# k and v from batch 3 on with four tokens to a partition: 40 k-v matmuls of mostly 128 rows in place of 72 of 64 rows

## The chip, the cores and the metric

The kernel runs on one core of one Trainium2 chip. The metric is the device time of one execution in microseconds (us); smaller is better. Executions that agree are called fast runs; one execution of the kernel before took 524 us and is left out of every comparison.

## The reference, cut to what matters

```python
# q, k, v: (8 batches, 8 heads, 576 tokens, 64)
q_s = softmax(q, over the 64 features)
k_s = softmax(k, over the 576 tokens)
kv  = einsum('bhsd,bhse->bhde', k_s, v)       # the k-v products
out = einsum('bhsd,bhde->bhse', q_s, kv)
# then out, as 4608 x 512, goes through silu(x @ w_in) @ w_out, w_in 512 x 2048
```

The k-v products are small: 64 by 64 per head. Most of the work is in the two large products behind them.

## The kernel before

The large products run by a scheme of seven products for eight, for which VectorE forms sums and differences of operand blocks (the tiles S, T, XS, WS, and GT in place). One batch of attention is worked into each stage of 26 us of large products: ScalarE takes exponentials of q and k, GpSimd casts v to bf16 (into `vaug`, which has a column for the softmax sum) and normalises q, a DMA transposes q (tile qT), TensorE makes the k-v products (`kv`) and later multiplies q with them (`xt`).

A load brings four heads as two pairs. Head r of a pair lies on partitions 64 r to 64 r + 63, nine tokens to a partition. So a k-v product contracts 64 partitions and runs on a quarter (64 rows by 64 columns) of TensorE's array:

```python
P, J = 64, S // 64                      # 64 partitions per head, 9 tokens each
x = src[b].rearrange("(g r) (p j) d -> g (r p) (j d)", r=2, j=J)
eng.dma_start(out=t, in_=x.rearrange("g x y -> x g y")[:, 2 * cc:2 * cc + 2, :])
...
def kv(b, cc):                          # cc: which half of the heads
    for j in range(J):
        for r in range(2):              # row half of the array
            for s in range(2):          # column half of the array
                nc.tensor.matmul(
                    out=PS[s * 64:(s + 1) * 64, 6 + r, cc * 128:cc * 128 + E1],
                    lhsT=ek[r * 64:(r + 1) * 64, j, (2 * cc + s) * D:(2 * cc + s + 1) * D],
                    rhs=vaug[r * 64:(r + 1) * 64, j, 2 * cc + s, :],
                    start=(j == 0), stop=(j == J - 1))
```

That is 9 x 2 x 2 = 36 matmuls for each half of the heads, 72 a batch.

The softmax here doesn't subtract the row's maximum and nothing guards it: scores larger than these inputs give would overflow.

Of the kernel before, what the change touches and what calls it, by code (L numbers as in the profile page):

```python
# [11 lines left out]
ACT = mybir.ActivationFunctionType  # L12
# [5 lines left out]
def kernel(  # L18
# [9 lines left out]
    nc = tc.nc  # L28
    B, H, S, D = q.shape
    DM, DFF = w_in.shape  # L30
    NT = B * S
    P = 64
    J = S // P
# [8 lines left out]
    E1 = D + 1  # L42
# [24 lines left out]
    vaug = glob.tile([128, J, NG, E1], BF16, name="vaug")  # L67
    ek = glob.tile([128, J, NG * D], BF16, name="ek")
# [5 lines left out]
    PS = ps.tile([128, 8, 512], FP32, name="PS")  # L74
# [10 lines left out]
    st = [dict() for _ in range(B)]  # L85

    def copy(eng, o, i):
        if eng is nc.scalar:
            eng.copy(out=o, in_=i)  # L89
        else:  # L90
            eng.tensor_copy(o, i)  # L91

    def load(b, name, src, cc, eng):
        t = ld.tile([128, 2, J * D], FP32, name=name)
        st[b][name, cc] = t
        x = src[b].rearrange("(g r) (p j) d -> g (r p) (j d)", r=2, j=J)
        eng.dma_start(out=t, in_=x.rearrange("g x y -> x g y")[:, 2 * cc:2 * cc + 2, :])

    def jgd(b, name, cc):
        return st[b][name, cc].rearrange("p g (j d) -> p j g d", d=D)  # L100

    def half(t, cc):
        return t[:, :, cc * 128:(cc + 1) * 128].rearrange("p j (g d) -> p j g d", d=D)
# [6 lines left out]
        )  # L110

    def exp_k(b, cc):
        nc.scalar.activation(out=half(ek, cc), in_=jgd(b, "kt", cc), func=ACT.Exp)  # L113

    def vcast(b, cc, eng, g0=0, g1=2):
        o = vaug[:, :, 2 * cc + g0:2 * cc + g1, 0:D]
        i = jgd(b, "vt", cc)[:, :, g0:g1, :]
        copy(eng, o, i)
# [66 lines left out]
    def kv(b, cc):  # L185
        for j in range(J):
            for r in range(2):
                for s in range(2):
# [4 lines that stand above are left out]
                        start=(j == 0),  # L193
                        stop=(j == J - 1),
                    )

    def kvcopy(b, c0=0, c1=2):
        kp = PS[:, 6:8, 0:256].rearrange("p r (c x) -> p r c x", x=128)[:, :, c0:c1, 0:E1]
        rz = ap.tile([128, 2, 2], FP32, name="rz", bufs=2)[:, :, 0:c1 - c0]
        nc.vector.reciprocal(out=rz, in_=kp[:, :, :, D])  # L200
        for c in range(c0, c1):
            nc.vector.tensor_tensor(
                out=kvn[b % 3][:, c],
                in0=kp[:, :, c - c0, 0:D],
                in1=rz[:, :, c - c0, None].to_broadcast([128, 2, D]),
                op=ALU.mult,
            )

    def kv_both(b):
        kv(b, 0)  # L210
        kv(b, 1)
        kvcopy(b)

    def pieces(t):
# [315 lines left out]
    for name, src in (("qt", q), ("kt", k)):  # L530
        load(0, name, src, 0, nc.sync)
        if name == "qt":
            load(0, name, src, 1, nc.sync)
    load(0, "vt", v, 0, nc.sync)
    load(0, "kt", k, 1, nc.sync)
    load(0, "vt", v, 1, nc.sync)
# [38 lines left out]
    qnorm(0, 0, nc.vector)  # L575
    qsum(0, 1)
    exp_k(0, 0)
    tr(0, 0, 0, 5, 0)
    tr(0, 0, 5, J, 1)
    heat(7)  # L580
    qnorm(0, 1, nc.vector)
    vcast(0, 0, nc.scalar)
    trcopy(0, 0, 0, 5, 0, nc.scalar)
    trcopy(0, 0, 5, J, 1)
    kv(0, 0)
    kvcopy(0, 0, 1)
    tr(0, 1, 0, 5, 2)
    tr(0, 1, 5, J, 3)
    exp_k(0, 1)
    xt_mm(0, 0, 0, 320, 4, 0)  # L590
    xt_mm(0, 0, 320, 256, 0, 0)
    heat(3, 6)
    vcast(0, 1, nc.scalar, 0, 1)
    vcast(0, 1, nc.vector, 1, 2)
    trcopy(0, 1, 0, 5, 2, nc.scalar)
    trcopy(0, 1, 5, J, 3)
    kv(0, 1)
    kvcopy(0, 1, 2)
    heat(2, 3)
    xt_evac(0, 0, 4, 0, 320, 0, nc.scalar)  # L600
# [47 lines left out]
    def full(t):  # L648
# [17 lines left out]
        for i in range(2):  # L666
            plan(u + (3, 10)[i], lambda i=i: exp_q(b, i))
            plan(u + (7, 11)[i], lambda i=i: qsum(b, i))
            plan(u + (16, 17)[i], lambda i=i: qnorm(b, i, nc.gpsimd))
            plan(u + (2, 11)[i], lambda i=i: vcast(b, i, nc.gpsimd))  # L670
            plan(u + (6, 4)[i], lambda i=i: exp_k(b, i))
            if more:
                plan(u + (5, 12)[i], lambda i=i: load(b + 1, "qt", q, i, nc.sync))
                plan(u + (8, 6)[i], lambda i=i: load(b + 1, "kt", k, i, nc.sync))
                plan(u + (22, 23)[i], lambda i=i: load(b + 1, "vt", v, i, nc.sync))
        plan(u + 17, lambda: q_transpose(b))
        plan(u + 15, lambda: kv_both(b))
        plan(u + 22, lambda: xt(t + 1, 0, nc.vector))
        plan(u + 27, lambda: xt(t + 1, 1))
# [98 lines left out]
    plan(b1 + 5, lambda: (vcast(1, 1, nc.scalar, 0, 1), vcast(1, 1, nc.vector, 1, 2)))  # L778
    plan(b1 + 6, lambda: (trcopy(1, 1, 0, 5, 0, nc.scalar), trcopy(1, 1, 5, J, 1)))
    plan(b1 + 7, lambda: kv_both(1))  # L780
    plan(b1 + 8, lambda: xt(1, 0))
    plan(b1 + 9, lambda: xt(1, 1))
# [20 lines left out]
    plan(b1 + 13, lambda: ws_op(1, 0))  # L803
    plan(b1 + 24, lambda: ws_op(2, 0))
    plan(b1 + 25, lambda: kv_both(2))
    plan(b1 + 24, lambda: t_op(2, nc.vector))
    plan(b1 + 27, lambda: xt(2, 0, nc.vector))
# [42 lines left out]
```

## Time and profile before

| what | before |
|---|---|
| median of its four runs, the 524 us run among them | 263.19 us |
| span of the profiled run | 260.8 us |
| TensorE busy | 252.4 us, 97% |
| VectorE busy | 207.3 us, 79% |
| one stage of large products, batches 4 to 7 | 26.2 us |
| the 72 k-v matmuls inside it | 0.83 us |

How to read it: TensorE is the bound, and work added to it in a stage without gaps moves the end by as much. The lines that show this stand in the prediction. Two more views of before are needed later. First the timeline in the stretch where batch 3 arrives (start us, length us, engine, line, operation, out<-in; the bracket is the idle time before and what ended it):

```profile
64.18 2.12 POOL L91 CAST vaug<-vt 128x1152 bf16<-128x1152 f32 x1 [9.03 <-DMA vt<-in_v_dram]
66.62 1.17 POOL L91 CAST vaug<-vt 128x1152 bf16<-128x1152 f32 x1 [0.32 <-DMA vt<-in_v_dram]
...
64.06 1.22 DVE L452 TENSOR_TENSOR W<-W 128x2048 f16<-128x2048 f16 x1
...
68.89 1.23 DVE L442 TENSOR_TENSOR S<-S,GT 128x2048 f16<-128x2048 f16 x1
```

GpSimd's casts of v follow their loads at once. VectorE's operations with two SBUF inputs take 1.22 us.

Second, the windows view of the loads' stretch (window, length, busy times of PE, PEld (weight loads), DVE (VectorE), ACT (ScalarE), POOL (GpSimd), clock, DMA share, GB/s):

```profile
59.00:67.00 8.00, 7.88 (x67) 5.64 (x66) 7.90 (x12) 7.39 (x10) 2.50 (x2) 1.00 1.04 388
```

The transfers run at 388 GB/s with every DMA engine taken.

### The profile page before, as it was taken

To read this page: it belongs to the slowest core of one execution; us is meant where nothing else is said; L and a number is where in the kernel's file an instruction comes from. 1 tells how busy PE (TensorE), PEld (TensorE's weight loads), DVE (VectorE), ACT (ScalarE), POOL (GpSimd) and SP (SyncE) were. 2 spreads that over 40 slices of the span, in tenths; PEclk is the share of its full clock that TensorE was granted. 3 is DMA by queue.
4 is the path that set the end of the run, shared out by engine and by line. 5 is a ranking of instruction groups with operands and counts; after the bars stand their busy time and mean duration, and the time that the engine had idled before them with its cause. 6 is when DMAs were issued, how large, how long until landed. Compare 5 with 4: busy or idle time off the path is not lost.

```text
span 260.8 us, 6412 instructions
## 1 busy us (share of the span) xinstructions
PE 252.4 (97%) x2732; PEld 203.0 (78%) x2732; DVE 207.3 (79%) x268; ACT 187.6 (72%) x212; POOL 66.9 (26%) x62
## 2 busy tenths in 40 slices
PE   8799999999999999999999999999999999999993
PEld 3457756656887888888888888888888888888882
DVE  2967786879997999799979997999798548855832
ACT  5767877998994799579956996699664757584710
POOL 1753691741360306030603060306000000000004
PEclk9999999999999999999999999999999999999999
DMA  7999999689979477957784879640424002500534
GB/s 248 334 198 298 298 323 333 253 186 384 309 284 222 123 209 247 197 146 201 258 220 118 214 249 152 182 104 3 90 61 102 3 0 46 117 3 1 120 84 121
DMA packets 35452, 45.89 MB, mean 176 GB/s; under 512 B 16208, under 2 KB 19984, under 8 KB 35424
## 3 DMA queue, kind: packets, MB, share of 16 engines
q1 hardware_dynamic: 29488, 33.63, 47.2%
q0 software_dynamic: 5616, 11.60, 16.9%
q8 instruction: 21, 0.34, 0.5%
q10 hardware_dynamic: 320, 0.26, 0.4%
q14 instruction: 7, 0.06, 0.1%
HBM read 36.70 MB, written 9.44 MB: 177 GB/s over the span
## 4 chain that ended last, share of the span: by engine, by line
PE 80%; DVE 12%; ACT 2%; POOL 2%; DMA 1%; issue 1%; POOLq 0%; DVEq 0%; ACTq 0%
PE PS L468 34%; PE PS L368 32%; PE PS L405 5%; PE PS L258 3%; PE PS L228 2%; DVE zq L148 2%; PE PS L189 2%; DVE h L346 2%; DMA qt<-in_q_dram 1%; PE PS L276 1%; DVE eq L157 1%; DVE GT L442 1%; DVE S L442 1%; ACT eq L108 1%; POOL out_dram L730 1%
## 5 line engine op out<-in xcount | busy, mean ns | idle before, releaser
L346 DVE TENSOR_TENSOR h<-PS,h 128x1024 f32<-128x1024 f32 (+1 forms) x45 | 53.9, 1199 | 12.0 <-PE PS L368 6.0
L468 PEld LDWEIGHTS <-GT 128*128 128x128 f16 x512 | 49.5, 98 | 6.9 <-issue 1.2
L368 PEld LDWEIGHTS <-WS 128*128 128x128 f16 x480 | 46.8, 98 | 7.5 <-issue 1.4
L468 PE MATMUL PS<-W,GT 128*128 128x256 f16 x384 | 49.1, 273 | 0.0
L368 PE MATMUL PS<-XS,WS 128*128 128x256 f16 (+1 forms) x360 | 46.3, 272 | 0.6 <-DVE h L346 0.5
L352 ACT ACTIVATE GT<-h 128x1024 f16<-128x1024 f32 (+1 forms) x45 | 46.1, 1047 | 0.3 <-DVE h L346 0.3
L89 ACT COPY h<-PS 128x1024 f32<-128x1024 f32 (+1 forms) x35 | 35.1, 1003 | 13.9 <-PE PS L368 13.4
L157 POOL TENSOR_TENSOR eq<-eq,rzq 128x1152 bf16<-128x1152 bf16 x13 | 27.7, 2134 | 57.6 <-DVE rzq L152 56.1
L468 PEld LDWEIGHTS <-S 128*128 128x128 f16 x384 | 37.1, 98 | 5.5 <-issue 1.0
L368 PEld LDWEIGHTS <-W 128*128 128x128 f16 x360 | 34.7, 98 | 4.8 <-issue 0.5
L468 PE MATMUL PS<-T,S 128*128 128x256 f16 x256 | 32.7, 273 | 0.1
L368 PE MATMUL PS<-XT,W 128*128 128x256 f16 (+1 forms) x240 | 29.5, 272 | 0.1
L352 ACT ACTIVATE GT<-PS 128x1024 f16<-128x1024 f32 (+1 forms) x15 | 15.2, 1016 | 18.9 <-PE PS L368 18.9
L91 POOL CAST vaug<-vt 128x1152 bf16<-128x1152 f32 x12 | 15.8, 1322 | 43.3 <-DMA vt<-in_v_dram 41.1
L730 POOL DMA_DIRECT2D out_dram<-ow x5 | 2.7, 546 | 72.1 <-DVE ow L715 72.1
L108 ACT ACTIVATE eq<-qt 128x1152 bf16<-128x1152 f32 (+1 forms) x18 | 19.0, 1057 | 2.5 <-DMA qt<-in_q_dram 2.4
L113 ACT ACTIVATE ek<-kt 128x1152 bf16<-128x1152 f32 x16 | 18.4, 1153 | 1.2 <-DMA kt<-in_k_dram 1.2
L148 DVE TENSOR_REDUCE zq<-eq 128x18 f32<-128x1152 bf16 x12 | 16.1, 1344 | 3.8 <-ACT eq L108 3.8
L258 PE MATMUL PS<-XT,W 128*128 128x288 f16 x128 | 16.3, 286 | 0.5 <-DVE XT L91 0.2
L468 PE MATMUL PS<-W,S 128*128 128x256 f16 x128 | 16.5, 273 | 0.0
L488 DVE SCALAR_TENSOR_TENSOR ow<-PS,sc 128x512 f32<-128x512 f32 x7 | 4.8, 691 | 14.4 <-ACT sc L484 14.4
L258 PEld LDWEIGHTS <-W 128*128 128x128 f16 x128 | 12.4, 98 | 4.3 <-issue 1.3
(78 smaller groups left out, 346.0 us busy)
## 6 DMA issues: line engine op xcount, KB each, us to landing
out_dram<-ow SPq DMA_DIRECT2D x64, 128.0 KB, 2.4
qt<-in_q_dram SPq DMA_DIRECT2D x12, 576.0 KB, 4.4
kt<-in_k_dram SPq DMA_DIRECT2D x12, 576.0 KB, 5.5
vt<-in_v_dram SPq DMA_DIRECT2D x12, 576.0 KB, 5.4
qt<-in_q_dram POOLq DMA_DIRECT2D x4, 576.0 KB, 10.3
kt<-in_k_dram POOLq DMA_DIRECT2D x4, 576.0 KB, 13.9
vt<-in_v_dram POOLq DMA_DIRECT2D x4, 576.0 KB, 13.2
W<-in_moe_w_out_dram POOLq DMA_DIRECT2D x4, 512.0 KB, 15.0
```

The costliest lines, as they stand in the source:

```text
L89: eng.copy(out=o, in_=i)
L91: eng.tensor_copy(o, i)
L108: nc.scalar.activation(out=half(st[b]["eq"], cc)[:, :, g0:g1], in_=jgd(b, "qt", cc)[:, :, g0:g1], func=ACT.Exp)
L113: nc.scalar.activation(out=half(ek, cc), in_=jgd(b, "kt", cc), func=ACT.Exp)
L148: nc.vector.reduce_sum(out=z, in_=e, axis=AX.X)
L157: eng.tensor_tensor(out=e, in0=e, in1=r[:, :, :, None].to_broadcast([128, J, 2, D]), op=ALU.mult)
L258: nc.tensor.matmul(out=PS[:, 2 * (fb % 3) + n, 0:S // 2], lhsT=W1[:, c, fb * 128:(fb + 1) * 128], rhs=XTS[0][:, c, n * (S // 2):(n + 1) * ...
L346: nc.vector.tensor_tensor(out=four(t, i), in0=group_bank(t, True), in1=four(t, i), op=ALU.add)
L352: nc.scalar.activation(out=group_out(t, f, n), in_=x, func=ACT.Silu, scale=1.0 / XS)
L368: nc.tensor.matmul(out=PS[:, bank + p // 2, (p % 2) * HT:(p % 2) * HT + width(t)], lhsT=a[:, c, p * 128:(p + 1) * 128], rhs=bb[:, c, 0:wid ...
L405: nc.tensor.matmul(out=PS[:, 2 + tb, :], lhsT=GTS[t % 2][:, fc, tb * 128:(tb + 1) * 128], rhs=W2[:, fc, :], start=(fc == 0), stop=(fc == N ...
L468: nc.tensor.matmul(out=PS[:, bank, m * HN:(m + 1) * HN], lhsT=a[:, fc, m * 128:(m + 1) * 128], rhs=bb[:, fc, :], start=(first and fc == 0) ...
```

## The change

The intent is fewer TensorE instructions: with a head's tokens over all 128 partitions, four to a partition, a product contracts 128 rows. 576 is 4 x 128 + 64, so the last 64 tokens of each head stay on 64 partitions: per half of the heads 4 x 4 wide matmuls and 4 narrow ones. Only batches 3 to 7 change.

```diff
+    JT = S // 128
+    def tall(b):
+        return b >= 3
     def load(b, name, src, cc, eng):
...
+        if tall(b) and name != "qt":
+            f = flat(t)
+            x = src[b][4 * cc:4 * cc + 4]
+            eng.dma_start(
+                out=f[:, 0:4 * JT * D].rearrange("p (h x) -> p h x", h=4),
+                in_=x[:, 0:JT * 128, :].rearrange("h (p j) d -> p h (j d)", j=JT),
+            )
+            x = x[:, JT * 128:S, :].rearrange("(g r) p d -> r p g d", r=2)
+            for r in range(2):
+                eng.dma_start(
+                    out=f[r * P:(r + 1) * P, 4 * JT * D:].rearrange("p (g d) -> p g d", g=2),
+                    in_=x[r],
+                )
+            return
...
+    def kv_tall(cc):
+        for j in range(JT + 1):
+            for r in range(2):
+                for s in range(2):
+                    rows = slice(0, 128) if j < JT else slice(r * P, (r + 1) * P)
+                    i = cc * 2 * J + ((2 * s + r) * JT + j if j < JT else 4 * JT + s)
+                    nc.tensor.matmul(
+                        out=PS[s * 64:(s + 1) * 64, 6 + r, cc * 128:cc * 128 + E1],
+                        lhsT=flat(ek)[rows, i * D:(i + 1) * D],
+                        rhs=vslot(i)[rows],
+                        start=(j == 0),
+                        stop=(j == JT),
+                    )
```

The exponentials of k and the casts of v run in flat order over the same 1,152 elements (cut here).

More of the change, by code (lines that the diff above doesn't have):

```diff
@@ L91, in copy, with flat @@
             eng.tensor_copy(o, i)
+    JT = S // 128
+    def tall(b):
+        return b >= 3
+    def flat(t):
+        return t.rearrange("p a b -> p (a b)")
     def load(b, name, src, cc, eng):
@@ L112, in exp_k, with vslot @@
     def exp_k(b, cc):
+        if tall(b):
+            nc.scalar.activation(
+                out=flat(ek)[:, cc * J * 128:(cc + 1) * J * 128],
+                in_=flat(st[b]["kt", cc]),
+                func=ACT.Exp,
+            )
+            return
         nc.scalar.activation(out=half(ek, cc), in_=jgd(b, "kt", cc), func=ACT.Exp)
+    def vslot(i):
+        return vaug.rearrange("p j g e -> p (j g) e")[:, i, :]
     def vcast(b, cc, eng, g0=0, g1=2):
+        if tall(b):
+            o = vaug.rearrange("p j g e -> p (j g) e")[:, cc * 2 * J:(cc + 1) * 2 * J, 0:D]
+            copy(eng, o, flat(st[b]["vt", cc]).rearrange("p (i d) -> p i d", d=D))
+            return
         o = vaug[:, :, 2 * cc + g0:2 * cc + g1, 0:D]
@@ L195, in kv @@
                     )
+    def kv_tall(cc):
[10 more added lines that the diff above has]
+                        stop=(j == JT),
+                    )
     def kvcopy(b, c0=0, c1=2):
@@ L209, in kv_both @@
     def kv_both(b):
-        kv(b, 0)
-        kv(b, 1)
+        for cc in range(2):
+            if tall(b):
+                kv_tall(cc)
+            else:
+                kv(b, cc)
         kvcopy(b)
```

## The prediction

> **What bounds the kernel now.** I read the page first (busy shares, chain of waits), then the windows view by stage, then the timeline around one batch's k-v products, then the waits.
>
> ```profile
> PE 252.4 (97%) x2732; PEld 203.0 (78%) x2732; DVE 207.3 (79%) x268; ACT 187.6 (72%) x212; POOL 66.9 (26%) x62
> ...
> PE 80%; DVE 12%; ACT 2%; POOL 2%; DMA 1%; issue 1%; POOLq 0%; DVEq 0%; ACTq 0%
> PE PS L468 34%; PE PS L368 32%; PE PS L405 5%; PE PS L258 3%; PE PS L228 2%; DVE zq L148 2%; PE PS L189 2%; DVE h L346 2%; DMA qt<-in_q_dram 1%; PE PS L276 1%; DVE eq L157 1%; DVE GT L442 1%; DVE S L442 1%; ACT eq L108 1%; POOL out_dram L730 1%
> ```
>
> TensorE is busy 97% of the span and is 80% of the chain that ended last. L189, the line that the change touches, has 2% of that chain, for eight batches. Five of them (3 to 7) change. So even taking their products away altogether is worth under 2%.
>
> The windows view, with the columns PE, PEld, DVE, ACT, POOL, then clock, DMA share and GB/s, shows where a TensorE saving or loss counts:
>
> ```profile
> 76.00:81.00 5.00, 4.51 (x82) 3.89 (x70) 4.97 (x7) 3.67 (x4) 1.61 (x1) 1.00 0.60 137
> 81.00:102.40 21.40, 21.40 (x205) 18.33 (x203) 19.11 (x23) 17.27 (x18) 5.28 (x4) 1.00 0.77 218
> 102.40:128.60 26.20, 26.20 (x313) 22.65 (x312) 23.76 (x29) 21.19 (x22) 6.56 (x5) 1.00 0.75 199
> 128.60:154.80 26.20, 26.20 (x313) 22.65 (x312) 23.76 (x30) 21.19 (x22) 6.56 (x5) 1.00 0.72 201
> ```
>
> From 81 us on, TensorE has no gap in a stage of 26.20 us: what is added to it there comes out at the end. In 76 to 81 us VectorE is the full engine. The chain in order of time says the same of batch 3's stage:
>
> ```profile
> 76.06 2.63 DVE GT L442
> 79.22 1.22 DVE h L346
> 80.48 1.03 PE PS L368 x8
> ```
>
> Batch 3's products run at 75.59 us, inside this VectorE stretch; the matmul at 80.48 had waited 0.49 us for VectorE (timeline). That batch can lose some 0.5 us on TensorE free of charge. The products of batches 4 to 7 lie at about 102, 129, 155 and 181 us, where TensorE is the bound.
>
> Now the stage itself, in the timeline (start, length, engine, what; the bracket is idle time before):
>
> ```profile
> 99.72 1.04 PE L368 MATMUL PS<-XT,WS 128*128 128x256 f16 x8
> ...
> 100.59 1.04 PE L468 MATMUL PS<-T,S 128*128 128x256 f16 x8
> ...
> 101.47 1.04 PE L368 MATMUL PS<-XT,W 128*128 128x256 f16 x8
> ...
> 102.43 0.69 PEld L189 LDWEIGHTS <-ek 64*64 64x64 bf16 x72 [0.21 <-issue]
> 102.43 0.81 PE L189 MATMUL PS<-vaug,ek 64*64 64x65 bf16 x72
> ```
>
> ```profile
> 103.17 1.05 PE L368 MATMUL PS<-XT,W 128*128 128x256 f16 x8
> 104.68 0.17 DVE L200 RECIPROCAL rz<-PS 128x4 f32<-128x4 f32 x1
> ```
>
> ```profile
> L189 PE MATMUL PS<-vaug,ek x576: 188/193/216, 10.9 to 181.6; 64*64 64x65 bf16 x192
> ```
>
> Groups of eight full matmuls start 0.875 us apart (99.72, 100.59, 101.47), which is 109 ns a matmul of 256 columns, or 0.43 ns a column. Without the products the next group would start at 102.34; it starts at 103.17. **So a batch's 72 products cost 0.83 us**, not 72 times their 193 ns. It splits in three. Entry: 102.34 to 102.43, 0.09 us. Stream: busy 0.81 less the last matmul's own 0.216 (the longest in the tile view) is 0.594 us from first start to last start, so 8.4 ns a matmul, or 33 ns for a round of four. Exit: the last starts at 103.03, streams 65 columns (65 x 0.43 = 28 ns) and the next group starts at 103.17, so 0.11 to 0.12 us. The 72 already run four abreast: 28 ns of streaming in a 33 ns round.
>
> **What the Trainium skill says.** "TensorEngine Tiling (Array Packing)", Key Properties: changing the tiling mode, "not just tile", drains the engine, and tiles work independently. The trace agrees with both: the 0.09 and 0.11 us at the ends, and four products in 33 ns. Its Available Configurations list 128x64 (two tiles) and 64x64 (four tiles) as separate modes; I take a step between them to be a mode change too, which nothing before the change shows. "TensorE: Matmul & The Clock Gate", Part 3, What overlaps and what doesn't: a weight load overlaps a matmul in flight only where the row group differs. The trace does not agree for the full-array matmuls: they use all rows, their loads have a median near 98 ns, yet they start every 109 ns, which is the stream alone. The new matmuls use all 128 rows as well, so I take their loads as hidden, with a doubt that I price below. "DMA: Bandwidth & Descriptors", Specifications, gives 512 B as the least transfer for line rate; no load before the change is in such small pieces, so no trace here shows what they cost.
>
> **The change, part by part.**
> (a) Matmuls. The order of instructions on each engine shows that TensorE loses 160 weight loads and 160 matmuls (32 in each of five batches) and that nothing else there moves. The 72 were 18 rounds of four 64x64 tiles. The new form has, for each half of the heads, 16 matmuls of 128 rows by 64 columns of the array, of which only two can be abreast: 8 rounds; then four of 64x64: 1 round. Two halves: 18 rounds. The array work is the same as before; the count falls only because each matmul takes twice the array. At 28 ns (stream alone) to 33 ns (round as now) the 16 wide rounds take 0.45 to 0.53 us, the two narrow ones 0.07: 0.52 to 0.60 us against 0.594. Saving per batch 0 to 0.07 us.
> (b) Mode steps. Before: into 64x64 and out of it. After: into 128x64, to 64x64, back to 128x64 for the second half, to 64x64, out. Three more, each some 0.10 us (the mean of 0.09 and 0.115): +0.30 us.
> (c) Sum per batch: +0.23 to +0.30, say +0.27 us. Batches 4 to 7 pay in full: 4 x 0.27 = 1.1 us. Batch 3 pays nothing, within its 0.49 us.
> (d) ScalarE's exponentials and GpSimd's casts have the same 1,152 elements a partition and the same count, only in flat order. Nothing. The products' result is read at 104.68, 1.4 us after they end: a late end does not show on VectorE.
> (e) Loads. Each of 20 k and v loads goes from one issue (256 pieces of 2,304 B) to three (512 pieces of 1,024 B, 256 of 256 B).
>
> ```profile
> 103.70 3.29 SPq L167 DMA_TRANSPOSE qT<-eq  x1
> 107.04 1.09 SPq L97 DMA_DIRECT2D vt<-in_v_dram  x2
> 114.09 6.09 SPq L401 DMA_DIRECT2D out_dram<-ow  x8
> ```
>
> An issue takes SyncE about 0.5 us (1.09 for two), so eight more in a stage are some 4 us on a queue that is busy about 15 of 26 us. Two v loads become six issues, 107.0 to 110.2, before the stores' 114.1. Landing now comes at 111.2 and 112.6, the casts follow at 111.3 and 112.8, and their reader is the next batch's products at 128.6: 14 us of slack. k loads are issued at 121 to 123 and read at 146. Both hidden. The tight place is batch 3's first loads: they are issued from 55 to 58 us in a stretch where the transfers are the limit, and the last of them, the second q half, lands at 67.9 and is read by ScalarE at 70.2. I estimate 0.3 us more for each of the four k and v loads before it, so 69.1: still in time, and perhaps 0.3 us if the semaphores that the issues share make SyncE wait. I put 0.2 us on it.
>
> Sum: 262.9 + 1.1 + 0.2 = **264.2 us**.
>
> **The rivals.**
> 1. *Fewer matmuls, less time* (the change's intent). If the 8.4 ns were a cost of issuing each matmul and not of the array, 40 would take 0.34 us and with no further mode cost each batch would save 0.25 us: 4 x 0.25, so 261.9 us. For it: 33 ns is more than the 28 ns of streaming, so issuing does bind a little. Against it: two wide matmuls abreast cannot stream 65 columns in less than 28 ns.
> 2. *Column halves don't overlap or weight loads show.* If the wide matmuls run one by one, 32 x 28 to 33 ns is 1.0 us in place of 0.53, so +0.5 on top of +0.3: 0.8 us in each of four or five batches, 266.3 us. If each weight load (64 columns, estimated at 28 ns like a stream) shows as well, 32 x 60 ns, +1.7 us a batch: 270 us. For it: the skill's sentence on row groups, and no 128x64 matmul in this trace. Against it: the full-array loads are hidden, and 64x64 tiles side by side on the same rows do overlap.
> 3. *The transfers become the bound* in 55 to 76 us, where the DMA share is 1.00 at the end. If small pieces take twice as long, the second q half is 2 to 3 us late, ScalarE waits, then VectorE: 265 to 267 us. For it: the small pieces. Against it: only a ninth of the bytes is in them, and later stages have a DMA share of 0.75 and over 10 us of slack.
>
> **Range and chances.** Rival 1 gives the low end, 261.9; half a miss of rival 2 or 3 gives the high end, 267. A gain over 2% (5.3 us) is impossible by the stage's whole cost of 5 x 0.83 = 4.2 us. A loss over 2% needs 1.3 us in each of four batches, which only unhidden loads or a bad stall reach: 6%.
>
> **What would show it.** The stage at batch 4: next full group 1.05 to 1.15 us later than it would start without the products, against 0.83 now, with breaks of about 0.1 us inside it between wide and narrow matmuls; wide ones 14 to 17 ns apart. A stage of about 26.5 us, not 26.2. Casts and exponentials of batches 4 to 7 still without a wait that TensorE feels. It is wrong if the inner breaks are absent (then the time falls), if the wide matmuls lie 30 ns or more apart (rival 2), or if ScalarE or VectorE waits on q, k or v near 66 to 76 us (rival 3).

## The result, and the profile after

The changed kernel took 264.97 us in the median of four runs (264.77 to 265.15). Ratios here are the mean time of one kernel's fast runs over that of the other's of the same rounds, so not quite the ratio of the medians quoted. The ratio is 1.0074, interval 1.0051 to 1.0098. Repeated in five rounds (e12 below), it was 264.88 against 263.23 us, ratio 1.0062, interval 1.0046 to 1.0078. So the change costs 1.6 to 2.0 us. It is slower, clear of noise, but by less than 1%.

The page of the changed kernel, busy line and chain by engine:

```profile
PE 254.7 (97%) x2572; PEld 204.2 (78%) x2572; DVE 207.9 (79%) x268; ACT 187.6 (71%) x212; POOL 66.3 (25%) x62
...
PE 84%; DVE 9%; ACT 2%; POOL 2%; DMA 1%; issue 1%; POOLq 0%; DVEq 0%; ACTq 0%
```

TensorE has 160 matmuls fewer and is busy 2.3 us more. Now the stage of batch 4 in the timeline, beside the lines of before in the prediction:

```profile
102.08 1.04 PE L423 MATMUL PS<-XT,W 128*128 128x256 f16 x8
103.05 1.13 PE L241 MATMUL PS<-vaug,ek 128*64 128x65 bf16 x40
104.11 1.05 PE L423 MATMUL PS<-XT,W 128*128 128x256 f16 x8
```

By the prediction's rule the next full group would have started at 102.08 + 0.875 = 102.95; it starts at 104.11. The products cost 1.16 us in place of 0.83. The single records of the stage give the starts of the 40 matmuls (ns from the first; computed from the trace):

```
16 wide, first half     0 .. 248     pairs: first to second 53 apart, then 29 to 36
4 narrow                373 .. 383   373 - 248 = 125 after the last wide one
16 wide, second half    528 .. 779   528 - 383 = 145 after the last narrow one
4 narrow                903 .. 913   903 - 779 = 124
before: 72 narrow       0 .. 593     rounds: first to second 53 apart, then 29 to 40; no break
```

So the matmuls themselves are no faster: a pair of wide ones takes what a round of four narrow ones took, 32 ns in the mean after the first step. And there are three breaks of 0.12 to 0.15 us, start to start, where an ordinary step is 0.03; before had none. First to last start, 0.913 us against 0.593: +0.32 us in a batch.

Following the products' start from batch to batch shows where the rest comes from (single records, us):

| batch | before | after | difference |
|---|---|---|---|
| 3 | 75.59 | 76.54 | +0.95 |
| 4 | 102.43 | 103.05 | +0.62 |
| 5 | 128.62 | 129.57 | +0.94 |
| 6 | 154.82 | 156.08 | +1.26 |
| 7 | 181.01 | 182.60 | +1.59 |
| a group of W,S matmuls near the end | 243.17 | 245.11 | +1.94 |

From batch 4 on, each stage adds 0.32 us, four times 1.3 us. The other 0.62 us is there before batch 4. At batch 3 it was 0.95, some of which the stage behind it took back. This 0.62 us rests on one trace of each kernel, and traces that load batch 3 in the old way differ among themselves: batch 4's products start at 102.30 us in e10, 102.43 in before, 102.83 in e1 and 103.08 in e5. The ratios of e2 and e6 below are the better evidence that batch 3 costs about half a microsecond. The timeline of the changed kernel shows what happened ahead of batch 3:

```profile
66.76 1.15 POOL L91 CAST vaug<-vt 128x1152 bf16<-128x1152 f32 x1 [11.60 <-DMA vt<-in_v_dram]
68.58 1.42 POOL L91 CAST vaug<-vt 128x1152 bf16<-128x1152 f32 x1 [0.66 <-DMA vt<-in_v_dram]
...
69.02 2.05 DVE L497 TENSOR_TENSOR S<-S,GT 128x2048 f16<-128x2048 f16 x1
...
71.12 1.05 PE L523 MATMUL PS<-T,S 128*128 128x256 f16 x8 [1.02 <-DVE S L497]
```

The casts come 2.6 and 2.0 us later than before, because v landed later. The second now runs beside VectorE's S operation, which takes 2.05 us in place of 1.23, and TensorE waits 1.02 us for it; its group starts at 71.12 us, where in before it started at 70.17. The loads' stretch in the windows view:

```profile
59.00:67.00 8.00, 7.88 (x68) 5.64 (x66) 7.90 (x12) 7.41 (x10) 0.24 (x1) 1.00 1.12 290
```

290 GB/s in place of 388, with the DMA engines as busy. The loads were also issued later. An issue is the instruction by which SyncE starts a transfer. Here are those of the two v loads in before, and below them in the changed kernel:

```profile
56.57 1.22 SPq L97 DMA_DIRECT2D vt<-in_v_dram  x2
...
59.48 0.52 SPq L109 DMA_DIRECT2D vt<-in_v_dram  x1
60.05 1.65 SPq L115 DMA_DIRECT2D vt<-in_v_dram  x2
61.86 0.48 SPq L109 DMA_DIRECT2D vt<-in_v_dram  x1
62.38 1.97 SPq L115 DMA_DIRECT2D vt<-in_v_dram  x2
```

Single records put the last v issue at 63.15 us, 5.9 us later than in before (57.27), and its landing at 68.43 us, 2.0 us later (66.47). A 32 KB issue of v took 4.4 us to land in this run's median. So, as an estimate, this one would have landed at about 67.5 us at the usual pace: SyncE's issuing may make half of the delay, the lower rate the rest. No run separates the two.

**How GpSimd can stop VectorE.** The Trainium skill, "SBUF — State Buffer", section "SBUF: two separate sides", says that VectorE and GpSimd share one pair of SBUF ports under an exclusive lock: a VectorE operation with two SBUF inputs and a GpSimd operation that reads SBUF exclude each other for the whole instruction, and the one that starts first gets it. The traces agree, in both directions. Alone, VectorE's 128x2048 operations of this kind take 1.22 us. Where GpSimd was already at work they ended 1.07 to 1.08 us after GpSimd's end, however long that took: 2.05 us (the S operation above), 2.35 and 2.71 us (the in-place GT operation of batch 3's stage, changed kernel and before). The lines of before for the last:

```profile
75.49 2.12 POOL L157 TENSOR_TENSOR eq<-eq,rzq 128x1152 bf16<-128x1152 bf16 x1 [1.49 <-ACT GT L352]
75.97 2.71 DVE L442 TENSOR_TENSOR GT<-GT 128x2048 f16<-128x2048 f16 x1
```

GpSimd ends at 77.61 us, VectorE at 78.68. And before's first cast, 0.12 us behind VectorE's W operation, took 2.12 us where others take 1.15.

### The profile page after: what moved, and what is told of

Read it like the earlier page. It is cut to its first block, busy times and chain, and to the rows that moved or that the text cites. A ratio compares the mean times of both kernels' runs of the same rounds, so it can differ in the third digit from the quotient of the medians.

```text
span 263.2 us, 6154 instructions
## 1 busy us (share of the span) xinstructions
PE 254.7 (97%) x2572; PEld 204.2 (78%) x2572; DVE 207.9 (79%) x268; ACT 187.6 (71%) x212; POOL 66.3 (25%) x62
## 4 chain that ended last, share of the span: by engine, by line
PE 84%; DVE 9%; ACT 2%; POOL 2%; DMA 1%; issue 1%; POOLq 0%; DVEq 0%; ACTq 0%
PE PS L523 35%; PE PS L423 33%; PE PS L460 5%; PE PS L313 3%; PE PS L283 2%; PE PS L241 2%; DMA qt<-in_q_dram 1%; DVE S L497 1%; PE PS L331 1%; DVE eq L195 1%; DVE zq L186 1%; ACT eq L132 1%; PE PS L227 1%; POOL out_dram L785 1%; DVE XT L91 1%
## 5 line engine op out<-in xcount | busy, mean ns | idle before, releaser
L91 POOL CAST vaug<-vt 128x1152 bf16<-128x1152 f32 x12 | 15.0, 1255 | 52.1 <-DMA vt<-in_v_dram 46.2
L460 PE MATMUL PS<-W,GT 128*128 128x512 f16 x64 | 15.6, 379 | 0.0
```

What stands on the lines that cost most here:

```text
L91: eng.tensor_copy(o, i)
L460: nc.tensor.matmul(out=PS[:, 2 + tb, :], lhsT=GTS[t % 2][:, fc, tb * 128:(tb + 1) * 128], rhs=W2[:, fc, :], start=(fc == 0), stop=(fc == N ...
```

## The experiments

**Theory A**: mode steps inside the products cost 0.32 us in each of batches 4 to 7, and late v loads cost batch 3 some 0.6 us through the port. Rivals: all from the loads (B), all from the matmuls (C), the new matmuls slow in themselves (D), the long S operation not caused by the cast (E). A mode step is a change from one tile shape of the array to another. "The S operation" is the second of the two that VectorE makes near 69 us. A gain or loss in us is the ratio less one, times the median of before; landing times and starts with three places are single records of the trace. Kernels e1 to e4 ran on one chip, e5 to e8 on a second, e9 to e12 on a third, each beside runs of before.

### e1: new matmuls on old loads

```diff
-        if tall(b) and name != "qt":
+        if False and name != "qt":
```

> The changed kernel's 40 matmuls on tiles that the old loads fill (wrong values on purpose: tokens of two heads are mixed; the work on every engine but the load queue is that of the changed kernel). Theory A (mode steps on TensorE cost the batches 4 to 7 some 0.32 us each, the smaller load pieces cost the rest through batch 3): batch 3's products start at 75.6 us again, no wait for VectorE at 70 us, each stage of batches 4 to 7 is 26.5 us, the sum +1.3 us over the kernel before, so about 264.2 us. Rival B (the loads make the whole loss, the matmuls none): equal to the kernel before, 262.9 us. Rival C (the matmuls make the whole loss): +1.8 us, 264.9 us.

Measured: ratio 1.0054 (1.0034 to 1.0075), 264.51 against 263.12 us, so +1.4 us. First to last start was 0.913 us again and the stages of batches 4 to 7 took 26.515 us each. The S operation took 1.23 us; batch 3's products started at 75.99 us and batch 4's at 102.83, 26.83 us later, as long as before (26.85), so batch 3's own 0.32 us was swallowed by VectorE's stretch, as predicted. B falls: the matmuls alone cost most of the loss. C's +1.8 us lies inside the interval (0.9 to 2.0 us), near its upper end; this run alone does not exclude it, e2 and e6 speak against it.

### e2: new loads under the old matmuls

```diff
         for cc in range(2):
-            if tall(b):
-                kv_tall(cc)
-            else:
-                kv(b, cc)
+            kv(b, cc)
```

> The changed kernel's loads, exponentials and casts with the old 72 matmuls of 64x64 (wrong values on purpose: the tokens lie elsewhere than these matmuls take them from; the time is unaffected by values). Theory A: the products' stage is 0.59 us from first to last start and a full stage 26.2 us, but VectorE's S operation near 69 us is held up by GpSimd's cast again and batch 3's products start near 76.5 us; +0.5 to +0.6 us over the kernel before, 263.4 us. Rival B: +1.8 us. Rival C: no loss.

Measured: ratio 1.0021 (1.0004 to 1.0038), +0.55 us. The products' first to last start was 0.585 us, the later stages 26.17 us, and the S operation took 2.05 us, all as A says. The profiled run was its slowest, 265.88 us (the others 263.4 to 264.1): in it, TensorE also waited 2.1 us for batch 3's transposed q. So the loads can hurt at a second place. The recorded ratio is about that of the six other runs; with the profiled run in, the plain mean is 0.9 us over before's. By the ratios e1 and e2 together make 1.95 us, the loss of the whole change, but with these intervals the agreement is a loose one.

### e3: the wide matmuls of both halves first, then the narrow ones

```diff
-    def kv_tall(cc):
-        for j in range(JT + 1):
+    def kv_tall(cc, js):
+        for j in js:
...
-                        start=(j == 0),
+                        start=(cc == 0 and j == 0),
...
+            for js in (range(JT), (JT,)):
+                for cc in range(2):
+                    kv_tall(cc, js)
```

(Only the first group in a bank may carry the start flag here, for both halves accumulate in the same banks at once.)

> The changed kernel with the order of its 40 matmuls altered: the 32 wide ones of both halves first, then the eight narrow ones, so one mode step inside in place of three; right values. Theory A (each inner step costs some 0.11 us): first to last start 0.68 us in place of 0.91, stages of 26.28 us in place of 26.52, about -1.1 us against the changed kernel, 263.9 us. Rival D (wide matmuls or narrow ones are slow in themselves, whatever their order): first to last start stays at 0.91 us and the time at 265.0 us.

Measured: right result, first to last start 0.691 us, stages of 26.274 us. The timeline of batch 4:

```profile
101.88 1.04 PE L426 MATMUL PS<-XT,W 128*128 128x256 f16 x8
102.85 0.89 PE L241 MATMUL PS<-vaug,ek 128*64 128x65 bf16 x40
103.67 1.05 PE L426 MATMUL PS<-XT,W 128*128 128x256 f16 x8
```

The same 40 matmuls in another order cost 103.67 - 102.76 = 0.91 us in place of 1.16. D falls: two breaks fewer make 0.22 to 0.25 us. The time, 264.48 us and ratio 1.0044 (1.0026 to 1.0063), is +1.2 us over before, where 263.9 us was expected. The profiled run, 263.61 us, was the fastest of six (the others 264.1 to 265.1). What the others lost is not in a trace.

### e4: no narrow matmuls

```diff
-                    rows = slice(0, 128) if j < JT else slice(r * P, (r + 1) * P)
+                    rows = slice(0, 128)
```

> The changed kernel with the eight narrow matmuls made wide too (wrong values on purpose: the last 64 tokens of two heads are mixed), so that there is no mode step inside at all. Theory A: 20 pairs at 31 ns, first to last start 0.62 to 0.65 us, stages of 26.25 us, 263.7 us. It also gives the price of a pair alone: were wide matmuls faster than the old 64x64 rounds, this would be below the old 0.59 us. Rival D (wide matmuls slow in themselves): 0.9 us or more.

Measured: first to last start 0.630 us, that is 20 pairs, 53 ns for the first step and 32 for the later ones in the mean; ratio 1.0024 (1.0008 to 1.0041), +0.6 us. No break is left inside, so the breaks come with the change of shape. It is not below the 0.593 us of before, but the comparison in the expectation is not a fair one: eight narrow matmuls made wide are four pairs in place of two rounds, so e4 streams 20 rounds where before and the change stream 18. Round for round the two are equal, 32 ns each. This is the answer to the change's intent: a pair of double size is no faster than four matmuls that run abreast.

### e5: only batches 4 to 7 changed; e6: only batch 3 changed

```diff
-        return b >= 3
+        return b >= 4        # e5;  b == 3 in e6
```

> The changed kernel with batch 3 left in the old layout and only batches 4 to 7 tall; right values. Theory A (the inner mode steps cost 0.32 us in each of batches 4 to 7, and batch 3's crowded loads cost about 0.5 us apart from them): batch 3's products start at 75.6 to 76.0 us, no wait for VectorE's S operation near 70 us, +1.3 us over the kernel before, 264.3 us. Rival C (TensorE alone makes the loss, and the late start of batch 3 is a matter of the single run): as the changed kernel, +1.8 us.

> Only batch 3 tall; right values. Theory A: batch 3's v lands 1.5 to 2 us later, GpSimd's cast meets VectorE's S operation, its products start near 76.5 us, its own 0.32 us are partly absorbed, and all later stages are 26.2 us: +0.5 to +0.6 us over the kernel before, 263.6 us. Rival C: +0.3 us at most.

Measured, e6: ratio 1.0017 (1.0001 to 1.0033), +0.45 us; the S operation 2.05 us; later stages 26.19 us. As A says. Its timeline also has the wait:

```profile
68.39 1.18 POOL L91 CAST vaug<-vt 128x1152 bf16<-128x1152 f32 x1 [1.18 <-DMA vt<-in_v_dram]
68.59 2.05 DVE L497 TENSOR_TENSOR S<-S,GT 128x2048 f16<-128x2048 f16 x1
...
70.70 1.05 PE L523 MATMUL PS<-T,S 128*128 128x256 f16 x8 [0.69 <-DVE S L497]
```

Measured, e5: ratio 1.0073 (1.0057 to 1.0089), +1.9 us, where 1.3 was expected: a miss. The S operations were short, the stages 26.515 us as expected, but batch 3's products started at 76.24 us. The timeline shows why:

```profile
63.82 1.22 POOL L91 CAST vaug<-vt 128x1152 bf16<-128x1152 f32 x1 [8.79 <-DMA vt<-in_v_dram]
...
63.94 2.17 DVE L507 TENSOR_TENSOR W<-W 128x2048 f16<-128x2048 f16 x1
...
67.30 1.03 PE L423 MATMUL PS<-XS,WS 128*128 128x256 f16 x8 [1.07 <-DVE h L401]
```

Here the first cast started 0.12 us *before* VectorE's W operation and so took the port; in the trace of before it was 0.12 us *behind* and lost it. This loss comes from nothing in the edit: batch 3's loads are the old ones. Whether the unprofiled runs of e5 lost the port too is not shown.

### e7: v ahead of the second k half in batch 3's loads

```diff
-        ("qt", q, 0), ("kt", k, 1), ("kt", k, 0), ("vt", v, 0), ("vt", v, 1), ("qt", q, 1)
+        ("qt", q, 0), ("kt", k, 1), ("vt", v, 0), ("vt", v, 1), ("kt", k, 0), ("qt", q, 1)
```

> The changed kernel with the first block of loads (batch 3) in another order: q, k half, v, v, k half, q, so that v lands 2 to 3 us earlier. Right values. Theory A: GpSimd's casts end before 67.5 us, VectorE's two S operations take 1.2 us each (1.5 and 2.05 in the changed kernel), the wait of 1.0 us on TensorE at 70 us is gone, batch 3's products start near 75.6 us, about -0.5 us against the changed kernel, 264.4 us. Rival E (the S operation is long for another reason than the cast beside it, such as the transfers' writes): it stays at 2 us and the time at 265.0 us.

Measured: the cast was out of the way, both S operations took 1.21 and 1.23 us, and batch 3's products started at 75.45 us, earlier than in before. The lines of e7:

```profile
64.45 3.03 POOL L91 CAST vaug<-vt 128x1152 bf16<-128x1152 f32 x2 [9.23 <-DMA vt<-in_v_dram]
67.51 1.21 DVE L497 TENSOR_TENSOR S<-GT 128x2048 f16<-128x2048 f16 x1
68.75 1.23 DVE L497 TENSOR_TENSOR S<-S,GT 128x2048 f16<-128x2048 f16 x1
```

E falls. But the time did not get better, where a gain of 0.5 us was expected: 265.18 against 262.65 us, ratio 1.0090 (1.0074 to 1.0106), a miss. What was won at 70 us was given back at 83 us:

```profile
82.73 0.28 PE L283 MATMUL PS<-qT,kvn 64*64 64x192 bf16 x4
83.73 0.33 PE L283 MATMUL PS<-qT,kvn 64*64 64x320 bf16 x4 [0.73 <-DMA qT<-eq]
```

Batch 3's transposed q landed at 83.7 us (82.3 in before). It shares the transfers with batch 4's k and q, whose last load landed at 81.7 us in place of 77.4 in before. So the slow loads set two limits for batch 3 that lie within a microsecond of each other, and removing the first uncovers the second.

### e8 and e11: before, with VectorE's GT operation moved out of GpSimd's way

```diff
-        for i, x in ((1, 4), (2, 5), (3, 15), (4, 19)):
+        for i, x in ((1, 4), (2, 5), (3, 18 if t == 2 else 15), (4, 19)):   # e8
```

> The kernel before, with one VectorE operation (the third S operation of the stage in which batch 3 is worked on) three units of work later, after GpSimd's second normalisation instead of beside it. Right values. If VectorE really stands still while GpSimd works on such an operation, it takes 1.22 us in place of 2.71 us, TensorE's wait of 0.49 us for VectorE near 80 us goes, and the kernel ends 0.3 to 0.5 us earlier than the kernel before: 262.5 us. If it doesn't, nothing changes, or TensorE waits for the late operation and it is slower.

Measured: the GT operation (the third S operation of the expectation) took 1.22 us in place of 2.71, but it now ran too late: TensorE waited 0.77 us for it in place of 0.49 for the h addition. Ratio 1.0025 (1.0005 to 1.0045): +0.65 us, a miss; the expectation had named this way to fail. e11 puts the same operation between the scaling of the products and the h addition:

> The kernel before, with batch 3's third S operation put behind the scaling of its k-v products in VectorE's queue instead of ahead of it, and ahead of the next h addition. Right values. VectorE then does the 0.7 us of scaling while GpSimd normalises, and waits less: the S operation takes about 1.5 us in place of 2.7, TensorE's wait of 0.49 us near 80 us shrinks to under 0.2, and the kernel is 0.3 to 0.4 us faster than before, 262.3 us, if the transpose of batch 3 is not the next limit; if it is, no change.

Measured: 262.94 against 263.23 us, ratio 0.9981 (0.9962 to 1.0): perhaps 0.5 us faster, not settled. Runs lie from 262.03 to 264.42 us. The profiled run was the slowest one; there the GT operation took 1.61 us as expected, but the whole run was 1.6 us late by 44 us, and the cast again got the port 0.08 us ahead of the W operation, which took 2.17 us.

### e9: old layout, loads cut into three issues

```diff
+        if b >= 3 and name != "qt":
+            eng.dma_start(out=t[:, 0], in_=y[:, 0])
+            for r in range(2):
+                eng.dma_start(out=t[r * P:(r + 1) * P, 1], in_=y[r * P:(r + 1) * P, 1])
+            return
```

> The kernel before, with each k and v load from batch 3 on cut into three issues as in the changed kernel (one of 128 partitions, two of 64), but still in pieces of 2,304 B. Right values. Theory F (the small pieces slow the transfers): batch 3's last v half lands near 66.5 us as before, the rate in 59 to 67 us stays near 390 GB/s, the time is that of the kernel before, 262.7 us. Rival G (the 20 times two more issues delay the loads): v lands near 68 us, VectorE's S operation is held up by the cast, and batch 4's second q half and the transpose come late as in the changed kernel: +0.5 us.

Measured: 267.43 against 263.23 us, ratio 1.0150 (1.0126 to 1.0174), +3.9 us, twice the loss of the change itself. But the four unprofiled runs had a granted clock of 0.991 to 0.992, before's 0.996 to 1.0; the profiled run, at 0.997, took 265.94 us, 2.7 us over before's median. So over a microsecond of the 3.9 may be of clock. The windows view and the timeline of the profiled run:

```profile
59.00:67.00 8.00, 7.88 (x68) 5.69 (x66) 7.90 (x12) 7.46 (x10) 0.00 (x0) 1.00 1.05 268
```

```profile
86.25 0.33 PE L234 MATMUL PS<-qT,kvn 64*64 64x320 bf16 x4 [2.56 <-DMA qT<-eq]
```

F as I put it falls: with the same 2,304 B pieces the rate drops to 268 GB/s when a load is cut into one issue over 128 partitions and two over 64. Both batch 3 effects appear, a long S operation (2.05 us) and a wait for the transpose. Cutting is enough to do the damage. It does not show that small pieces are harmless: in e9 half of the bytes go in the 64-partition issues, in the change a ninth does. And the issues come late in e9 too (the last of v at 62.86 us). How the delay of v divides between SyncE's issuing, the cutting and the piece size stays open.

### e10: grouped matmuls, batches 4 to 7 only

e3's order with `b >= 4`.

> The grouped order of matmuls (32 wide, then eight narrow, one inner step) and only batches 4 to 7 tall: the cheapest tall version that the findings allow. Right values. If the parts add up: stages of 26.27 us in place of 26.19, 4 x 0.08 = +0.3 us over the kernel before, 263.0 us. A loss of 1 us or more would say that something apart from mode steps and batch 3's loads costs time.

Measured: stages of 26.27 us, as expected. The profiled run took 263.16 us, the other five 264.16 to 264.72, ratio 1.0036 (1.0017 to 1.0056), +0.95 us. The trace agrees with the sum, the mean does not; the same gap as in e5. It would fit the port being lost in those runs, but no trace of them exists. Open.

### e12: the changed kernel again

> The changed kernel again, unaltered, for a closer interval on the same chip as the three others: +1.8 us over the kernel before. If its loss is TensorE's four stages of +0.32 us and batch 3's +0.6 us: 264.6 us.

Measured: 264.88 us, ratio 1.0062, first to last start 0.912 to 0.914 us, the S operation 2.05 us, TensorE's wait for it 0.8 us. The first trace was no exception.

No version beat both kernels clear of noise.

## Why the prediction was right or wrong

The time, 264.97 us, lies inside the range and 0.8 us above the predicted 264.2. The direction held, and so did the reason for most of the loss. That the sum came so close owes something to luck: the part for the loads, 0.2 us, was estimated for another wait than the one that came.

- **Part (a), no gain from fewer matmuls**: right, in size too. Wide pairs come every 32 ns in the mean, inside the 28 to 33 predicted, as the rounds of four did before. Eighteen rounds of the changed kernel without breaks would take 53 + 16 x 32 + 10 ns (the last round's own spread), some 0.575 us: an estimate from the recorded starts, 0.02 below the 0.593 of before, where 0 to 0.07 was predicted. The intent's hope (rival 1) fell with it.
- **Part (b), three more mode steps of 0.10 us**: right in its mechanism, a little too small. All three together make 0.913 less 0.575, 0.34 us, where 0.30 was predicted. e3 takes two of them away and gets 0.22 us back, also 0.11 each.
- **Part (c), the sum per batch**: the mechanism was right, the term was mis-sized: +0.27 predicted, +0.32 measured, most of the difference in the steps of part (b). Four batches: 1.3 us, not 1.1. Batch 3's own 0.32 was absorbed in e1 as predicted.
- **Part (d), "Nothing" for the casts**: this step failed. Their own work did not change, but their place in time did, and by the shared port it matters to VectorE when GpSimd works.
- **Part (e), loads, 0.2 us**: mis-sized and wrong in its mechanism. I had looked at whether the last q half would be late for ScalarE; it landed at 69.66 us, where 69.1 was predicted, still in time for 70.18. What happened was that v was late (68.4 us in place of 66.5), the cast met the S operation, and TensorE waited 1.02 us; net 0.62 us. My own 0.3 us a load would have put v at about 67.7 us, but I did not ask what its cast meets then. And I counted SyncE's time for the added issues in the stages with slack, not in this tight place. I had also taken the transpose's margin for granted; e7 and e9 show it to be the next limit.
- **Rival 2** (column halves one by one, weight loads showing): not seen. Two wide matmuls start 3 to 4 ns apart, and the loads of 128 rows hide.
- **Rival 3** was the right suspicion with the wrong chain: the rate fell as feared, but through GpSimd and VectorE, not through a wait of ScalarE for q.

## What to carry to other kernels

Before cutting a count of matmuls, work out how many run abreast and how many columns the array must stream: 72 quarter-array matmuls and 32 half-array plus 8 quarter-array ones are the same 18 rounds. Count changes of the tile shape instead, which cost some 0.11 us each here, and keep equal shapes together. And when a load changes shape, follow its landing to the engine that consumes it and ask which other engine that one can stop.

## What the Trainium skill lacked or had wrong

- "TensorEngine Tiling (Array Packing)", Key Properties: says that a change of mode drains the engine, without a price. Here 124 to 145 ns pass from the last matmul of one shape to the first of the next, where 32 ns pass between pairs of one shape in the mean; going from 128x64 to 64x64 counts as such a change.
- "TensorE: Matmul & The Clock Gate", Part 3, What overlaps and what doesn't: says that weight loads overlap matmuls in flight only if the row group differs. In e4 all 40 matmuls and their loads use all 128 rows, the loads have recorded lengths of 106 to 114 ns, and a pair still starts every 32 ns, so they overlap. (The section The mechanism, just above, does name a background weight buffer, so the page is not at one with itself.)
- "DMA: Bandwidth & Descriptors": the 512 B limit of its Specifications can't be tested by these runs. Its Rules for kernel authors do advise one transfer of 128 partitions in place of two halves, but without a price. Here a load was cut into one issue of 128 partitions and two of 64: with pieces of 2,304 B throughout, the rate went from 388 to 268 GB/s (e9).
- "SBUF — State Buffer", SBUF: two separate sides: the lock is as described, the order of arrival included. How long the blocked operation takes afterwards is not said: VectorE's ended 1.07 to 1.08 us after GpSimd's end, where it takes 1.22 us alone. Nor is how little decides it: 0.12 us one way or the other put a delay of 0.95 us on GpSimd (before) or on VectorE (e5).
